# A gated recurrence and a long convolution on one core: row-tiled transposes and single-bank PSUM outputs

## The chip, the cores and the metric

The kernel runs on one core of one Trainium2 chip. The metric is device time in microseconds (us) for one launch. The core has five engines that run their own instruction streams: TensorE (PE, matrix multiply, with its weight loads shown apart as PEld), VectorE (DVE), ScalarE (ACT), GpSimd (POOL) and SyncE (SP, which here issues all DMAs). Matmul results land in PSUM, 8 banks of 512 fp32 values in each of 128 partitions; PE alone writes matmul outputs there, and in this kernel ACT and DVE read ("evict") them. A weight load puts the stationary operand into PE's array. An operand of 64 rows takes one half of the array's rows, a "row tile"; two row tiles can work side by side.

## The reference

Four batches of 6272 steps and 256 channels; all inputs and the output are fp32.

```python
sig = 1 / (1 + exp(-f_logit))
f = lower_bound + (1 - lower_bound) * sig
i = 1 - f
for t in range(S):                       # per batch and channel
    h = f[:, t] * h + i[:, t] * x[:, t]
    y[:, t] = h
proj = y @ w_proj                        # 256 -> 768
x1, x2, x3 = proj[..., :D], proj[..., D:2*D], proj[..., 2*D:]
X2 = rfft(x2, axis=1)
H = rfft(filter_fft, axis=0)
x2_conv = irfft(X2 * H, axis=1)
out = (x1 * x2_conv * x3) @ w_out
```

## The kernel before

The sequence of 6272 is split as 128 x 49, and the Fourier transforms are done as matmuls with small tables: a transform over 128, then one over 49, with the twiddles folded into a shifted table. The work of one batch has these steps, each with the name that the code gives its operations:

- `hgrn(b)`: 13 chunks of 512 steps (the last 128). A chunk's `x` and `f_logit` are loaded with time on the partitions, four blocks of 128 steps. ACT makes the sigmoid in place (`sig`, line 392), POOL multiplies `u = x * sig` in place (`u`, line 394), PE transposes both to channels on the partitions (`sT` of the gate, `uT` of u, line 401), for each half `kh` of the channels apart. ACT turns the transposed gate into f (`f`, line 415), and DVE runs the recurrence with a scan instruction that reads f from SBUF and u from PSUM (`scan`, line 423). A copy of the first 3072 steps is put behind the end (`wrap`).
- `phase_p`: x2, projected straight into the order that the transform needs (`P`, line 730; evicted by `x2`, line 733).
- `phase_f1`: the transform over 128, units of 8 channel pairs, 16 units a batch (`F1`, line 743; evicted by `A`, line 746). `mini` does the same few rows of all units at once.
- `unit`: the transform over 49 in two row tiles of 64 (`F2`, line 788), the product with the filter's spectrum on DVE (`prod`, line 801, two an unit, one for each of the two banks o = 0, 1), a small POOL add (`slot`), and the inverse over 49 (`I2`, line 811; evicted by `Th`, line 816).
- `gate`: x1 and x3 in 13 chunks and two halves of the channels (`x13`, line 450), copied to SBUF by ACT (`xs`, line 462) and multiplied on POOL into `zt` (`z`, line 466).
- `phase_o`: 13 groups of four of the 49 residues (the last group one): the inverse over 128 in two row tiles (`I1`, line 844), the product with `zt` on DVE (`y`, line 850), the output projection (`proj`, line 862), its eviction (`o`, line 868) and the store.

A preparation ahead of the first batch makes the tables and the filter's spectrum with the same two transforms (`rot`, `FF1` at line 672 with its eviction `afs`, `FF2`), and runs `hgrn(0)` beside them. `hgrn(b+1)` is put in after `phase_o(b)` in the program, and its operations mix with those of batch b.

The order of all instructions is not the program's order. Each step calls `op(...)`, which records an operation with its inputs and outputs, the engines that may do it with a cost in us for each, and, for a matmul group, the number of neighbouring PSUM banks that it takes (`take`). `Plan.schedule` then lists the operations by simulated time: it takes the operation that could start earliest, with ties by `levels` (the longest way to the end) plus two hand-set tables, `LEAD` and `TILT`; `SHY` adds a delay to an engine's offer for a kind of operation. `ROWS` names the kinds that run in row tiles, and `STICK` makes PE prefer to stay on one side. A bank is free again when all readers of the operation that took it are done, or, where the readers name a `part`, bank by bank. `either(n)` offers ACT and DVE for an eviction of n elements a partition. At run time every engine runs its list in order, and waits on semaphores for data and banks.

Of the kernel before, what the change touches and what calls it, by code (L numbers as in the profile page):

```python
# [10 lines left out]
F32R = mybir.dt.float32r  # L11
F16 = mybir.dt.float16
I32 = mybir.dt.int32
AOP = mybir.AluOpType
# [43 lines left out]
class Plan:  # L58
# [14 lines left out]
    SHY = {("A", "ACT"): 27, ("A", "DVE"): 27, ("Th", "ACT"): -10, ("Th", "DVE"): 779,  # L73
            ("afs", "ACT"): 51, ("afs", "DVE"): -12, ("f", "ACT"): -4, ("f", "DVE"): 452,
            ("f2", "ACT"): 100, ("f2", "DVE"): 126, ("fr", "ACT"): 290, ("fr", "DVE"): 2705,
            ("fr", "POOL"): -84, ("hw", "ACT"): -32, ("hw", "DVE"): 364, ("o", "ACT"): 13,
            ("o", "DVE"): 1968, ("wrap", "ACT"): 1376, ("wrap", "POOL"): 115, ("x2", "ACT"): 90,
            ("x2", "DVE"): 63}

    STICK = 4.0  # L80
    ROWS = ("F2", "mini", "I1", "FF2", "last")
# [3 lines left out]
        "A": (10, -421, 208, -185), "F1": (-87, -1, 1, -163), "F2": (297, -97, -22, -362),  # L85
        "FF1": (-72, 0, 0, 0), "FF2": (-79, 0, 0, 0), "H": (-184, 334, 22, 133),
        "I1": (-280, -65, -92, 13), "I2": (-282, -43, -206, 0), "P": (-10, -2, 64, -49),
        "Th": (-3, -372, 21, -100), "afs": (-31, 0, 0, 0), "f": (-348, -382, -7, -601),
        "f2": (206, 0, 0, 0), "ff": (-455, 0, 0, 0), "fr": (-21, 0, 0, 0), "hst": (-91, 0, 0, 0),
        "hw": (11, 0, 0, 0), "load": (-7, -238, -192, 0), "mX": (18, 0, 0, 0),  # L90
        "mini": (-412, 357, -19, 94), "o": (0, -19, 214, 0), "pad": (14, 0, 0, 0),
        "prod": (0, -199, -22, 1135), "proj": (387, -1338, -11, 254), "rot": (-287, 0, 0, 0),
        "sT": (-25, 1516, -37, 149), "scan": (-40, -6, -71, -138), "sig": (-116, 262, -46, -451),
        "slot": (-6, -10, -78, 18), "store": (-23, -498, 174, 242), "tabs": (335, 0, 0, 0),
        "u": (-6, 0, -48, 383), "uT": (-1369, -27, 23, 104), "warm": (-427, 0, 0, 0),
        "wrap": (0, 312, 253, 2), "x13": (-140, -373, -471, -159), "x2": (35, -288, 339, 160),
        "xs": (2160, 1264, 0, 301), "y": (-27, 470, 49, -42), "z": (0, 0, 532, 756),
        "zm": (1130, 0, -12, 65),
# [3 lines left out]
        "A": (35, -373, 1648, 137), "F1": (462, -629, 1502, 4000), "F2": (5639, 140, 319, 1412),  # L102
        "FF2": (-1269, 0, 0, 0), "H": (0, -477, -796, -1751), "I1": (-67, 978, 15, 184),
        "I2": (-35, -8, 4207, 55), "P": (-34, -342, 3292, -57), "Th": (164, 540, 125, 0),
        "args": (598, 0, 0, 0), "f": (294, -69, -69, -264), "f2": (-491, 0, 0, 0),
        "ff": (5684, 0, 0, 0), "fr": (505, 0, 0, 0), "hst": (566, 0, 0, 0), "hw": (-475, 0, 0, 0),
        "iden": (346, 0, 0, 0), "iota": (33, 0, 0, 0), "last": (43, 0, 0, 0),
        "load": (1910, -587, 70, -424), "mX": (103, 0, 0, 0), "mini": (162, -443, 3560, 2034),
        "o": (182, 252, -11, 418), "pad": (-134, 0, 0, 0), "pre": (-656, 0, 0, 0),
        "prod": (53, -700, 0, 7), "proj": (-7749, -9436, -6234, 114), "rest": (109, 0, 0, 0),  # L110
        "sT": (0, -96, -2, -1), "scan": (-892, 17, -1191, -2973), "sig": (0, 79, 43, 146),
        "slot": (126, 219, 502, 1379), "store": (-387, -299, -79, -369), "tabs": (5294, 0, 0, 0),
        "turns": (-46, 0, 0, 0), "u": (801, 3, 107, 648), "uT": (10, -692, -6798, -121),
        "warm": (-40, 0, 0, 0), "wcol": (443, 0, 0, 0), "wl": (-474, 0, 0, 0),
        "wrap": (-936, -549, -39, 333), "x13": (-350, -2412, -46, -1943), "x2": (0, 0, 1048, 2601),
        "xs": (5528, -104, 106, -88), "y": (-100, -570, -30, -285), "z": (-742, -2, 69, 0),
        "zm": (236, 148, 847, -6),
# [41 lines left out]
    def schedule(self, level):  # L159
# [14 lines left out]
        base = {}  # L174
# [13 lines left out]
        while base:  # L188
            rooms = {n: self.room(bank, n) for n in (1, 2)}
            best = None  # L190
            for i, b in base.items():
# [8 lines left out]
                for e, a in b.items():  # L200
                    a = max(a, floor, free[e])
                    c = a + (o["cost"][e] * 0.01 if len(b) > 1 else 0.0)
                    c += self.SHY.get((o["kind"], e), 0) / 100
                    stick = self.STICK if e == "PE" and (o["kind"] in self.ROWS) == rows else 0.0
                    key = (c, -level[i] - stick, i, e, a)
                    if best is None or key < best:
                        best = key
# [32 lines left out]
            for j in inform.get(i, ()):  # L240
                wait[j] -= 1
            for j in o["succ"]:
# [35 lines left out]
def kernel(  # L278
# [65 lines left out]
    def At(u):  # L344

        return [("At", u % NA)]
# [33 lines left out]
    def hgrn(b):  # L380
        for c in range(NCHK):
# [6 lines left out]
            for dst, src, t in ((ft, f_logit, ("ft", k)), (xt, x, ("xt", k))):  # L388
# [5 lines left out]
            op("u", {"POOL": 0.1 + 0.553 * nb}, lambda e, xt=xt, ft=ft: nc.gpsimd.tensor_tensor(  # L394
                xt, xt, ft, op=AOP.mult), r=[("ft", k)], w=[("xt", k)])
            for kh in range(2):
# [537 lines left out]
```

## Time and profile before

| | |
|---|---|
| five runs | 503.39 to 510.31 us, median 506.26 |
| profiled execution | 507.04 us, of which the span from the first to the last instruction is 505.2 |
| mean granted PE clock | 0.991 of full speed |
| DMA | 116.39 MB, 230 GB/s on average over the span |

| group, by line | count | mean ns | busy us |
|---|---|---|---|
| L466 POOL z (128x490) | 96 | 1983 | 189.0 |
| L801 DVE prod | 128 | 1198 | 146.7 |
| L394 POOL u (128x1024) | 48 | 2384 | 114.3 |
| L423 DVE scan (128x512) | 96 | 1270 and 1218 | 120.2 |
| L401 PE transposes, 128x128 f32 | 784 | 283 and 276 | 124.7 |
| L401 PE weight loads for them | 784 | 142 | 90.9 |
| L862 PE projection, 128x256 | 392 | 292 | 59.2 |
| L862 PE weight loads for it | 392 | 188 | 49.6 |
| L850 DVE y (128x1024) | 48 | 1216 | 58.0 |
| L415 ACT f (128x512) | 96 | 694 | 66.6 |
| L462 ACT x1s and x3s (128x490) | 192 | 591 | 113.3 |
| L462 ACT x1s and x3s (128x392) | 16 | 508 and 506 | 8.1 |
| L361 ACT Th (128x784) | 64 | 824 | 52.7 |
| L363 ACT o (128x1024) | 48 | 1024 | 49.0 |
| L361 ACT A (128x1024), L366 DVE A | 46, 18 | 1024, 1216 | 46.9, 21.6 |
| L361 ACT f2, L366 DVE f2 (128x512, strided read of PSUM) | 13, 11 | 688, 697 | 7.8, 7.1 |
| L366 DVE afs (128x512) | 32 | 677 | 20.8 |
| L707 PE weight loads (64x98 fp32r) | 8 | 162 | 0.5 |

How to read it: a row's mean is the time from an instruction's start to its modelled end, while the next one on the engine may already have started, above all on PE, where a row of 283 ns does not mean that PE is taken for 283 ns. In the chain of waits an instruction counts only until the next in the chain starts. "L450 <- L811" style releasers are inferred from semaphore events. PEclk is the granted clock; it stood at full speed from 90 us on.

### The profile page before, as it was taken

What the parts mean: (1) busy time and instruction counts of PE and PEld (TensorE: products, weight loads), DVE (VectorE), ACT (ScalarE), POOL (GpSimd) and SP (SyncE); (2) the same over time, 40 slices, a digit from 0 to 9 for tenths busy, and PEclk for the clock granted to TensorE, in tenths of its full rate; (3) what the DMA queues carried; (4) which work ended last, traced back from release to release, by engine and by line L of the source; (5) the groups of instructions that cost most, each with busy time, mean ns of one, the idle gap of its engine ahead of it and who ended that gap; (6) DMA issues with size and microseconds to landing.
All of it is one profiled execution on the core that took longest, in us unless ns stands there. A gap on an engine that the chain in (4) does not pass through costs nothing. (4 is left out here: it accounts for less than half of the span.)

```text
span 505.2 us, 13245 instructions
## 1 busy us (share of the span) xinstructions
PE 479.7 (95%) x5257; PEld 374.5 (74%) x5257; DVE 444.0 (88%) x451; ACT 411.5 (81%) x587; POOL 386.1 (76%) x328
## 2 busy tenths in 40 slices
PE   7979998999999999999998999999999999999795
PEld 6768785866777899867766889767778888666484
DVE  8789997789899999899996989989999978989773
ACT  3657867889999877899898787899989777999654
POOL 8886766789999864499999867789998732997900
PEclk9998999999999999999999999999999999999999
DMA  8969999616668999247678899056788970344166
GB/s 331 407 216 287 322 309 302 208 39 217 219 204 272 280 321 393 96 134 215 194 212 273 290 328 361 9 172 205 242 284 300 334 281 28 97 128 133 62 240 272
DMA packets 41725, 116.39 MB, mean 230 GB/s; under 512 B 4384, under 2 KB 6304, under 8 KB 41664
## 3 DMA queue, kind: packets, MB, share of 16 engines
q1 hardware_dynamic: 41664, 115.56, 67.6%
q8 instruction: 41, 0.67, 0.6%
q14 instruction: 20, 0.16, 0.1%
HBM read 84.54 MB, written 31.00 MB: 229 GB/s over the span
## 5 line engine op out<-in xcount | busy, mean ns | idle before, releaser
L466 POOL TENSOR_TENSOR zt<-x1s,x3s 128x490 f16<-128x490 f32 (+1 forms) x104 | 201.8, 1954 | 42.6 <-ACT x3s L462 26.1
L801 DVE TENSOR_TENSOR PP<-PS,Hu 98x1008 f16<-98x1008 f32 x128 | 146.7, 1198 | 10.1 <-ACT x3s L462 3.3
L394 POOL TENSOR_TENSOR XT<-XT,FL 128x1024 f32<-128x1024 f32 (+1 forms) x52 | 117.2, 2257 | 34.5 <-DMA XT<-in_x_dram 13.5
L423 DVE TENSOR_TENSOR_SCAN HA<-fTs,HA,PS 128x512 f16<-128x512 f32 (+1 forms) x96 | 114.0, 1203 | 12.3 <-PE PS L401 8.2
L450 PE MATMUL PS<-HA,W 128*128 128x490 f16 (+1 forms) x416 | 107.8, 372 | 1.8 <-DVE PP L801 1.0
L415 ACT ACTIVATE fTs<-PS,nomc 128x512 f32<-128x512 f32 (+1 forms) x104 | 69.5, 669 | 19.9 <-PE PS L401 12.9
L850 DVE TENSOR_TENSOR ys<-PS,zt 128x1024 fp32r<-128x1024 f32 (+1 forms) x52 | 59.9, 1158 | 12.9 <-PE PS L844 8.0
L363 ACT ACTIVATE osb<-PS 128x1024 f32<-128x1024 f32 (+1 forms) x52 | 50.6, 977 | 20.3 <-PE PS L862 17.5
L401 PE MATMUL PS<-iden,XT 128*128 128x128 f32 x392 | 63.5, 283 | 3.2 <-ACT fTs L415 1.5
L462 ACT ACTIVATE x1s<-PS 128x490 f32<-128x490 f32 (+1 forms) x104 | 60.8, 585 | 5.8 <-PE PS L450 2.9
L462 ACT ACTIVATE x3s<-PS 128x490 f32<-128x490 f32 (+1 forms) x104 | 60.6, 584 | 3.9 <-POOL zt L466 2.1
L862 PE MATMUL PS<-Wo,ys 128*128 128x256 f32 x392 | 59.2, 292 | 2.9 <-DVE ys L850 1.7
L401 PE MATMUL PS<-iden,FL 128*128 128x128 f32 x392 | 61.2, 276 | 0.3 <-ACT FL L392 0.3
L811 PEld LDWEIGHTS <-PP 98*128 98x128 f16 x1024 | 50.1, 98 | 10.8 <-issue 2.4
L392 ACT ACTIVATE FL<-FL 128x1024 f32<-128x1024 f32 (+1 forms) x52 | 52.6, 1013 | 6.1 <-DMA FL<-in_f_logit_dram 6.0
L401 PEld LDWEIGHTS PS<-iden,XT 128*128 128x128 f32 x392 | 45.1, 142 | 15.7 <-POOL XT L394 2.6
L361 ACT CAST Th<-PS 128x784 f16<-128x784 f32 x64 | 52.7, 824 | 4.6 <-PE PS L811 4.2
L450 PEld LDWEIGHTS <-W 128*128 128x128 f16 x416 | 35.2, 99 | 28.1 <-issue 10.3
L862 PEld LDWEIGHTS PS<-Wo,ys 128*128 128x128 f32 x392 | 49.6, 188 | 7.1 <-DVE ys L850 2.2
L811 PE MATMUL PS<-VA,PP 98*128 98x98 f16 x512 | 52.4, 207 | 1.5 <-DVE PP L801 0.7
L811 PE MATMUL PS<-VB,PP 98*128 98x98 f16 x512 | 52.1, 207 | 0.0
L366 DVE CAST X<-PS 128x1024 f16<-128x1024 f32 (+1 forms) x34 | 46.9, 1476 | 5.2 <-PE PS L730 3.9
(98 smaller groups left out, 699.9 us busy)
## 6 DMA issues: line engine op xcount, KB each, us to landing
Hu<-H SPq DMA_DIRECT2D x64, 392.0 KB
FL<-in_f_logit_dram SPq DMA_DIRECT2D x48, 512.0 KB
XT<-in_x_dram SPq DMA_DIRECT2D x48, 512.0 KB
out_dram<-osb SPq DMA_DIRECT2D x48, 512.0 KB
X<-in_moe_filter_fft_dram SPq DMA_DIRECT2D x9, 512.0 KB
H<-Hu SPq DMA_DIRECT2D x16, 196.0 KB
H<-Hu SPq DMA_DIRECT2D x16, 128.0 KB
Hu<-in_moe_filter_fft_dram SPq DMA_DIRECT2D x2, 512.0 KB
```

Of the source, the lines that this page charges most:

```text
L361: nc.scalar.copy(dst, src)
L394: op("u", {"POOL": 0.1 + 0.553 * nb}, lambda e, xt=xt, ft=ft: nc.gpsimd.tensor_tensor(xt, xt, ft, op=AOP.mult), r=[("ft", k)], w=[("xt", k)])
L401: nc.tensor.transpose(PS[:, p, j:128 * nb:nb], src[:, j, cols], iden[:])
L415: nc.scalar.activation(fT, PS[:, p, 0:n], AF.Identity, scale=by, bias=1.0)
L423: nc.vector.tensor_tensor_scan(h, fT, PS[:, p, 0:n], init, op0=AOP.mult, op1=AOP.add),
L450: nc.tensor.matmul(PS[:, p, 0:n], W13[:, kh, js], HA[:, HB[kh] + t0:HB[kh] + t0 + n], start=(kh == 0), stop=(kh == 1))
L462: nc.scalar.activation(xs(i), PS[:, p, 0:n], AF.Copy, scale=1.0 if i else ZS),
L466: nc.gpsimd.tensor_tensor(late["zt"][:, jb, :, m0:m0 + nm], xs(0).rearrange("p (m r) -> p r m", r=Q), xs(1).rearrange("p (m r) -> p r m", ...
L801: nc.vector.tensor_tensor(PP[:TB, k, o, :, :, 1:64], px.unsqueeze(1).broadcast_to([TB, 2, UE, 63]), hh[:, :, :, 1:64], op=AOP.mult)
L811: nc.tensor.matmul(PS[:, ib + o, pr * TB:(pr + 1) * TB], PP[:TB, k, o, n, 2 * pr:2 * pr + 2, :], v[:TB], start=(n == 0), stop=(n == 1))
L850: nc.vector.tensor_tensor(late["ys"][:, yk, :, 0:rn * 128], PS[:, cb:cb + 2, 0:rn * 128], late["zt"][:].rearrange("p k r m -> p k (r m)") ...
L862: nc.tensor.matmul(po[:, i, :], late["ys"][:, yk, kh, i * 128:(i + 1) * 128], Wo[:, kh, :], start=(kh == 0), stop=(kh == 1))
```

## The change

It does the following.

- A 128x128 transpose is done as two of 64 rows (`turn`), one in each row tile, each with a 64x64 identity. One operation `sT` (and one `uT`) now serves both halves of the channels: it takes two neighbouring banks, the first row tile writes the last n columns of the first bank and the second row tile the first n of the second, and the halves of the channels interleave. `f` and `scan` read every second column of that run. `sT` and `uT` are added to `ROWS`.
- `F1`, `I2` and `proj` are split in halves of one bank each, with an eviction for each half. `A`, `Th` and `osb` get a token for each half, so a half of I2 needs only its own prod.
- `FF1`'s table `D1r` is no longer doubled; the matmuls stream 128 columns in place of 256, and a group takes one bank.
- `u` and `z` may be done by DVE as well as POOL, `xs` by DVE as well as ACT.
- The planner remembers for an operation that takes banks when its readers' other inputs are ready (`need`), and delays the operation's offer until its result is due then.
- The tables `SHY`, `TILT` and `LEAD` have new values, and so the order of the instructions is another one everywhere.

```diff
-    SHY = {("A", "ACT"): 27, ("A", "DVE"): 27, ("Th", "ACT"): -10, ("Th", "DVE"): 779,
...
+    JIT = 0.0
-    ROWS = ("F2", "mini", "I1", "FF2", "last")
+    ROWS = ("F2", "mini", "I1", "sT", "uT", "FF2", "last")
...
+                    if o["take"]:
+                        c = max(c, need[i] - o["cost"][e] - self.JIT)
...
             for j in inform.get(i, ()):
                 wait[j] -= 1
+                need[j] = max(need[j], end[i] + self.LAT[e])
...
-        return [("At", u % NA)]
+        return [("At", u % NA, h) for h in range(2)]
...
-            op("u", {"POOL": 0.1 + 0.553 * nb}, lambda e, xt=xt, ft=ft: nc.gpsimd.tensor_tensor(
+            op("u", {"POOL": 0.1 + 0.553 * nb, "DVE": 0.07 + 0.268 * nb}, lambda e, xt=xt, ft=ft: (nc.gpsimd if e == "POOL" else nc.vector).tensor_tensor(
                 xt, xt, ft, op=AOP.mult), r=[("ft", k)], w=[("xt", k)])
+            def run(p, at, m, step):
+
+                return PS[:, p:p + 2].rearrange("m a n -> m (a n)")[:, at:at + (m - 1) * step + 1:step]
+
+            def turn(e, p, src, nb=nb, n=n, run=run):
+                for j in range(nb):
+                    for kh in range(2):
+                        for a in range(2):
+                            rows = slice(64 * a, 64 * a + 64)
+                            nc.tensor.matmul(run(p, 512 - n + a * n + kh + 2 * j, 64, 2 * nb),
+                                             src[rows, j, kh * 128:kh * 128 + 128], iden[rows, rows],
+                                             is_transpose=True, start=True, stop=True)
+            sT = op("sT", {"PE": 0.125 * nb}, lambda e, p, f=turn, s=ft: f(e, p, s),
+                    r=[("ft", k), "iden"], w=["qT"], take=2)
+            uT = op("uT", {"PE": 0.125 * nb}, lambda e, p, f=turn, s=xt: f(e, p, s),
+                    r=[("xt", k), "iden"], w=["qT"], take=2)
             for kh in range(2):
-                def turn(e, p, src, cols=cols, nb=nb):
-                    for j in range(nb):
-                        nc.tensor.transpose(PS[:, p, j:128 * nb:nb], src[:, j, cols], iden[:])
-                sT = op("sT", {"PE": 0.109 * nb}, lambda e, p, f=turn, s=ft: f(e, p, s),
-                        r=[("ft", k), "iden"], w=["qT"], take=1)
-                uT = op("uT", {"PE": 0.109 * nb}, lambda e, p, f=turn, s=xt: f(e, p, s),
-                        r=[("xt", k), "iden"], w=["qT"], take=1)
...
-                        nc.scalar.activation(fT, PS[:, p, 0:n], AF.Identity, scale=by, bias=1.0)
+                        nc.scalar.activation(fT, run(p, at, n, 2), AF.Identity, scale=by, bias=1.0)
...
-                   nc.vector.tensor_tensor_scan(h, fT, PS[:, p, 0:n], init, op0=AOP.mult,
+                   nc.vector.tensor_tensor_scan(h, fT, run(p, at, n, 2), init, op0=AOP.mult,
...
-                    op("xs", {"ACT": 0.05 + n / 1200.0}, lambda e, p, xs=xs, n=n, i=i:
+                    op("xs", {"ACT": 0.05 + n / 1200.0, "DVE": 0.07 + n / 960.0}, lambda e, p, xs=xs, n=n, i=i:
...
-                op("z", {"POOL": 0.1 + 3.68 * n / 1000}, lambda e, xs=xs, jb=jb, m0=m0, nm=nm:
-                   nc.gpsimd.tensor_tensor(
+                op("z", {"POOL": 0.1 + 3.68 * n / 1000, "DVE": 0.08 + 1.7 * n / 1000},
+                   lambda e, xs=xs, jb=jb, m0=m0, nm=nm:
+                   (nc.gpsimd if e == "POOL" else nc.vector).tensor_tensor(
...
-        D1r = tmp.tile([128, 2, 128], F32R, name="D1r")
+        D1r = tmp.tile([128, 128], F32R, name="D1r")
...
-                        w=[("FF1", u, h)], take=2)
+                        w=[("FF1", u, h)], take=1)
...
-        f1 = op("F1", {"PE": 0.056 * UE}, mm, r=[("x2", g) for g in range(NX2)] + ["D1"], take=2)
-        k = u % NA * UE
-        op("A", either(1024), lambda e, pb: copy(
-            e, A[:, k:k + UE],
-            PS[:, pb:pb + 2].rearrange("p a (i r k) -> p (a i) r k", r=2, k=64)),
-           w=At(u), src=f1)
+        for h in range(2):
+            k = u % NA * UE + 4 * h
+
+            def mm(e, pb, j=u * UE + 4 * h):
+                for i in range(4):
+                    nc.tensor.matmul(PS[:, pb, i * 128:(i + 1) * 128], X2[:, (j + i) * PW:(j + i) * PW + 128],
+                                     D1[:], start=True, stop=True)
+            f1 = op("F1", {"PE": 0.224}, mm, r=[("x2", g) for g in range(NX2)] + ["D1"], take=1)
+            op("A", either(512), lambda e, pb, k=k: copy(
+                e, A[:, k:k + 4], PS[:, pb].rearrange("p (i r k) -> p i r k", r=2, k=64)),
+               w=[("At", u % NA, h)], src=f1)
...
-        i2 = op("I2", {"PE": 0.695}, inv,
-                r=[("P", k, 0), ("P", k, 1), ("Pz", k, 0), ("Pz", k, 1), "V"], take=2)
-        op("Th", either(784), lambda e, ib: copy(
+            i2 = op("I2", {"PE": 0.347}, inv, r=[("P", k, o), ("Pz", k, o), "V"], take=1)
+            op("Th", either(392), lambda e, ib, o=o: copy(
...
-            po = op("proj", {"PE": 0.259 * rn}, proj, r=[("y", yk)], take=2)
+            for i0 in range(0, rn, 2):
+                n = min(2, rn - i0)
...
+                po = op("proj", {"PE": 0.259 * n}, proj, r=[("y", yk)], take=1)
+                op("o", either(256 * n), lambda e, ob, k=k, i0=i0, n=n: copy(
```

## The prediction

> **What bounds the kernel now.** I read the page's first part, then the busy time by stage, then the chain of waits inside one stage, then the groups by shape. The columns of the stage table are us from the start, length, and busy us (x instructions) of PE, PEld, DVE, ACT and POOL, then clock, DMA share and GB/s. Its cuts are the first matmuls of each batch's P (line 730): preparation with the first recurrence, three middle stages (one batch's spectrum, gate and output, beside the next batch's recurrence), and a last stage with no recurrence beside it.
>
> ```profile
> PE 479.7 (95%) x5257; PEld 374.5 (74%) x5257; DVE 444.0 (88%) x451; ACT 411.5 (81%) x587; POOL 386.1 (76%) x328
> ```
>
> ```profile
> 0.00:90.20 90.20, 80.67 (x580) 63.58 (x581) 74.98 (x108) 61.58 (x84) 66.11 (x85) 0.96 0.90 312
> 90.20:200.40 110.20, 108.39 (x1245) 85.68 (x1244) 102.59 (x95) 96.93 (x141) 93.48 (x69) 1.00 0.71 235
> 200.40:307.50 107.10, 102.99 (x1195) 80.53 (x1194) 97.52 (x92) 90.75 (x132) 86.31 (x66) 1.00 0.70 228
> 307.50:414.10 106.60, 105.59 (x1227) 83.83 (x1226) 99.06 (x93) 93.64 (x137) 87.62 (x67) 1.00 0.68 234
> 414.10:505.20 91.10, 82.02 (x1018) 60.91 (x1016) 69.80 (x65) 68.62 (x96) 52.60 (x42) 0.99 0.41 142
> ```
>
> A busy PE is a modelled thing, so its prices come from the chain of waits in a stretch where PE alone is the chain (start, us, what):
>
> ```profile
> 379.68 0.87 PE PS L401 x8
> ...
> 382.61 1.01 PE PS L844 x32
> ...
> 386.49 0.56 PE PS L844 x16
> 387.04 1.02 PE PS L401 x8
> 388.07 0.95 PE PS L862 x8
> 389.01 0.56 PE PS L844 x16
> ```
>
> Eight transposes (L401) take 0.87, or 0.109 each. Sixteen more I1 matmuls (L844, two row tiles of 64) cost 1.01 - 0.56 = 0.45, or 0.028 each; what is left of 0.56 is 0.11, the price of leaving row tiles for the full array. Coming back costs 1.02 - 0.87 = 0.15 at most. A projection matmul is 0.95 / 8 = 0.118. The same chain gives P 0.109 (x98 in 10.74), x13 0.206 (x8 in 1.65), F1 0.056 (x24 in 1.34), F2 0.54 for eight with a switch in it, I2 0.044 (x16 in 0.70).
>
> PE's load in a middle stage, summed: P 98 x 0.109 = 10.7; x13 104 x 0.206 = 21.4; F1 128 x 0.056 = 7.2; F2 16 x 0.54 = 8.6; I2 256 x 0.044 = 11.3; I1 196 x 0.028 = 5.5; projection 98 x 0.118 = 11.6; transposes 196 x 0.109 = 21.4; together 97.7. The order of PE's records shows about 62 switches a stage, of which F2's 16 are already counted; 46 x 0.1 = 4.6. Sum 102 of 106.6 us: PE is 96% taken, so PE sets the middle stages. DVE and ACT stand close behind (99.1 and 93.6 us busy of 106.6).
>
> **The change part by part.** The sum is made against the profiled execution, 507.04 us (span 505.2 and 1.8 around it); the median of the five runs, 506.26, is 0.8 less.
>
> *Transposes.* A 128x128 transpose becomes two of 64 rows, in two row tiles and two banks. Per 128 rows of one tensor, two instructions of 0.109 become two pairs. What is a pair worth? The rows that bear on it:
>
> ```profile
> 82.48 0.71 PE L690 MATMUL PS<-afs,FTr 64*98 64x512 f32 x4
> 83.02 0.48 PE L707 MATMUL PS<-mX,FTr 64*98 64x128 f32 x8
> 83.44 0.66 PE L401 MATMUL PS<-iden,XT 128*128 128x128 f32 x4
> ```
>
> L707 is the nearest: fp32r in two row tiles, eight matmuls between 83.02 and 83.44. Less the switch of 0.1 that is four pairs in 0.32, so 0.08 a pair, though each loads its own weights of 98 columns and streams 128. Low bound: half as many streamed columns, 0.055 a pair. High bound: the load alone sets the 0.109 and doesn't shrink with half the rows, 0.109 a pair, gain nothing. Between them: the load row of L707 lasts 160 ns and its pair 83, of the projection 188 ns and its step 118, so a load row is 70 to 77 ns longer than what it costs; the transposes' load row is 142 ns, which leaves 65 to 72. I take 0.07 a pair: it comes from three rows of fp32 loads. A middle stage has 196 transposes, so 196 x (0.109 - 0.07) = 7.6 us of PE; by the bounds 0 to 10.6.
> The Trainium skill (TensorE: Matmul & The Clock Gate, "LDWEIGHTS") says the opposite of my choice: a load takes columns / 1.2 GHz whatever its rows, 107 ns for 128 columns, so the pair would stay at 0.107 and the gain at zero; L707's pair at 0.08 for 98 columns agrees with that rule as well as with mine.
>
> *Switches.* The transposes now stand on the row-tiled side. Counted in the same order of PE's records, a middle stage would have 78 to 88 switches in place of 62 to 64, +20 x 0.1 = 2 us; an order that groups them can avoid some. I take 1.6. Net of PE: 6 us a stage, to 96; at the same 96% share the stage would last 100.6.
>
> *F1, I2, projection in halves.* The same matmuls on PE, but 44 more evictions a batch (16 A, 16 Th, 12 o). ACT rows at two sizes give the fixed part: 490 elements 591 ns, 392 elements 506 ns (L462), so 0.87 ns an element and 165 ns fixed. The chain shows neighbours on ACT 0.47 apart where the row says 0.59, so only some 45 ns of that is lost between neighbours. 44 x 0.045 to 44 x 0.165 is 2 to 7 us, shared by ACT and DVE; I take 3. They stand idle for 13.0 and 7.5 us of the stage at 106.6, and what a shorter stage takes from that is the limit I give below. In return each half's reader starts a matmul group earlier, and the second half of I2 needn't wait for the first's eviction; that fills gaps, and I count it at nothing (0 to 1 us a stage).
>
> *Strided reads.* f and scan now read every second element of two banks. The nearest rows are the f2 copies, which read PSUM 256 elements apart: ACT 688 ns for 512 against 694 for the contiguous f, DVE 697 against 677 for afs. At most 20 ns x 26 on either engine, 0.5 us a batch; taken as zero. The strided write goes from every fourth to every eighth element; no row prices it, and it is inside the pair's bounds.
>
> *FF1.* 128 columns in place of 256. Its step is the load's, 0.118 as in L862, and L707's pairs show that 128 fp32r columns need no more than 0.08. Taken as zero, bounds -3 to +3 us in the preparation, where DMA (0.90 busy) and DVE hide it.
>
> *z, u and xs also on DVE.* POOL's z is 1983 ns and u 2384. On DVE, z is bounded by half a prod (1198 / 2 = 0.6) and by POOL's own 1.98; u is nearest to y (1216). In the middle stages DVE has no room to take many. The last stage is different:
>
> ```profile
> 473.84 3.33 POOL zt L466 x2
> 477.17 1.54 POOLq L929
> 478.73 1.24 DVE ys L850
> 480.00 1.21 PE PS L862 x8
> ```
>
> From 467.1 to 477.2 the chain is POOL's z, while PE is busy 11.0 of the 14 us from 466 to 480. DVE has 3.3 us free there. Taking a few z off POOL can bring the output forward by no more than PE's idle 3.0; I take 3 (0 to 4). The twelve output groups after it are PE's, I1 0.56 and projection 1.14, and stay.
> The skill (Advanced Engine Details and Errata, "GPSIMD Details") says that POOL shares a port with DVE and conflicts with DVE instructions of two SBUF inputs, which z and u on DVE would be; no DVE row here has two large SBUF inputs. By it, this part would be worth nothing.
>
> *Preparation.* The first recurrence saves the same 7.6 us of PE less switches, but DMA is 0.90 busy and DVE 75.0 of 90.2; I take 2 (0 to 5).
>
> *Sum.* 3 x 6 + 3 + 2 = 23: 507.0 - 23 = 484, on the median 483; I write 483.5.
>
> What is late next: DVE and ACT. Per stage they are busy 192.7 of 213.2 us; with 3 more and a stage of 100.6, 195.7 of 201.2. It just fits, because a busy row contains up to 0.12 us in which the next instruction already runs, and only if A, x2 and xs are spread evenly. If it doesn't fit, a stage saves 2 to 3 us, not 6.
>
> **The rivals.**
> *DVE and ACT take over.* For it: scans and y's alternate on DVE in the output stretch, 1270 + 1216 ns, against PE's group of 0.56 + 0.95 + 1.02 = 2.53, so there DVE is already level with PE and the transposes' gain is worth nothing in it. Against: recurrence and evictions can move between stretches. 3 x 2.5 + 2 = 9.5: 497.
>
> *The pair costs what the whole did.* A load of 128 columns sets the pace, PE saves nothing, switches cost 3 x 2 and the tail gives 3 back: 507 + 6 - 3 = 510. For it: the high bound above. Against: load rows of 142 for a step of 109.
>
> *Banks held longer: slower.* One chunk's sT and uT now hold two banks each until both of their readers are done; before, a bank was free after one reader. With I1's two and the projection's two, the eight are full: the next chunk's transposes can start only after the second scan, and DVE then waits for them: 8 pairs x 0.07 + 0.15 + about 0.1 of hand-over = 0.8 us a chunk (scans already wait on L401 0.63 on average, 8.8 us in 14 waits). It decides from 23 / 0.8 = 29 of the 52 chunks on, for then it has eaten the gain. With 45 chunks uncovered, +36 - 23: 520. Against: y (1.22) can stand between two chunks' scans, and sT's banks are free after two f of 0.69.
>
> **How the numbers follow.** Forecast 484: 0.66. Engines take over, 497: 0.12. Pair at full price, 510: 0.12. Banks, 520: 0.10. The forecast's own range: pairs at 0.055, no extra switches and 5 and 4 at the two ends make 3 x 9 + 9 = 36, so 471; 3 x 2.5 + 1 makes 498. The range that leaves out two in ten reaches over the second case and into the third: 470 to 507. A change of 1% is about what the runs can tell from none: faster 0.77, same 0.12, slower 0.11.
>
> **What would show it.** In the profile after: sixteen half transposes in about 0.56 us in the chain (0.44 or 0.87 would be the bounds); PE's share falling while DVE and ACT reach 95% of a middle stage; stages near 101 us; POOL's z gone from the chain before the last output. Wrong would be: scans waiting on L401 at most chunks; stages still at 106 with PE's row tiles at 0.109 a pair; or ACT's idle time before its evictions gone while PE waits for free banks.

## The result, and the profile after

| | before | after |
|---|---|---|
| median of the runs (lowest to highest, number) | 506.61 (503.39 to 510.31, 43) | 515.89 (506.35 to 523.13, 24) |
| ratio to before, 95% interval | | 1.0078 [1.0049, 1.0108] |
| profiled execution, and its span | 507.04, 505.2 | 514.09, 512.0 |
| mean granted PE clock of the profiled execution | 0.991 | 0.972 |

The change made the kernel slower, by 0.8% in the ratio and by 9 us in the medians; forecast were 483.5, and 470 to 507 as the range. The ratio leaves out the longest runs of after, in which the granted clock was lowest, so it is smaller than that of the medians, 1.018; the low clock turns out to be part of the change's effect. The page's busy row, the slices of PE and of its clock, after:

```profile
PE 466.2 (91%) x6041; PEld 352.4 (69%) x6041; DVE 453.0 (88%) x470; ACT 425.1 (83%) x758; POOL 363.4 (71%) x314
...
PE   8888987899799898999999979999999999999996
...
PEclk9996598999899999999999999999999999999999
```

PE is no longer at 95%, so something was taken off it; and the fourth and fifth slices, near 38 to 64 us, show a clock near half, which before did not have. The chain of waits after (start, us, what) shows what the transposes cost now:

```profile
47.62 1.90 PE PS L410 x32
...
306.87 1.01 PE PS L410 x32
...
336.52 0.98 PE PS L800 x16
337.50 0.49 PE PS L410 x16
338.00 1.35 PE PS L463 x6
```

Sixteen half transposes, eight pairs, take 0.49, or 0.061 a pair against 0.109 for the whole one before. At 47.62, in the slow stretch, 32 take 1.90, nearly twice the 1.01 of 306.87. The windows by stage, cut at the first matmul of each batch's P (start:end, length, busy us of PE, PEld, DVE, ACT, POOL, then clock, DMA share, GB/s):

```profile
0.00:94.30 94.30, 80.18 (x806) 62.12 (x806) 72.95 (x111) 66.78 (x93) 68.97 (x86) 0.87 0.87 304
94.30:206.80 112.50, 102.86 (x1400) 77.16 (x1400) 103.13 (x96) 96.94 (x178) 81.89 (x64) 0.98 0.69 227
206.80:318.00 111.20, 101.76 (x1431) 76.81 (x1430) 103.81 (x99) 96.48 (x179) 86.09 (x66) 1.00 0.70 231
318.00:421.10 103.10, 97.35 (x1370) 72.42 (x1369) 99.24 (x93) 92.31 (x171) 77.50 (x62) 1.00 0.70 222
421.10:512.00 90.90, 84.03 (x1042) 63.92 (x1038) 73.84 (x75) 72.62 (x140) 49.00 (x39) 0.99 0.43 151
```

Cut at the same places, before has 90.3, 105.6, 111.5, 106.5 and 91.2 us (the second cut of the prediction's table, 200.40, belongs at 195.9; the sum of the first two middle stages is hardly touched). So preparation lost 4.0, the first middle stage lost 6.9, the third gained 3.4, and the others stayed. PE is idle for some 9.5 us in each of the first two middle stages (before 1.8 and 4.1): the time that was taken off it became gaps.

Two things stand out. One is the clock: in the rows of 3.4 us from 45.4 to 62.4 it is at exactly half. The windows of one such row, before and after:

```profile
48.80:52.20 3.40, 3.35 (x26) 2.75 (x27) 3.05 (x5) 2.02 (x3) 2.25 (x3) 1.00 0.90 259
```

```profile
48.80:52.20 3.40, 3.40 (x26) 2.65 (x23) 2.63 (x3) 3.02 (x4) 1.82 (x4) 0.50 0.75 204
```

PE is just as "busy" in both; the busy row says nothing of the clock. In the whole profiled execution the half-speed stretches of after are 20.5 us from 42.7 and 3.4 each at 83.6 and 131.4; before has 3.4 each at 38.8 and 86.6 (both have one more at the end). The other thing is VectorE. Its timeline and that of POOL after, and a piece of the chain of waits farther on (start, us, engine, line, operation):

```profile
121.75 2.30 DVE L813 TENSOR_TENSOR PP<-PS,Hu 98x1008 f16<-98x1008 f32 x2
123.96 4.33 DVE L399 TENSOR_TENSOR XT<-XT,FL 128x1024 f32<-128x1024 f32 x1
128.21 1.27 DVE L436 TENSOR_TENSOR_SCAN HA<-fTs,HA,PS 128x512 f16<-128x512 f32 x1
```

```profile
122.70 0.65 POOL L376 COPY HA<-HA 128x512 f16<-128x512 f16 x1
123.27 3.93 POOL L479 TENSOR_TENSOR zt<-x1s,x3s 128x490 f16<-128x490 f32 x2
129.54 1.16 POOL L376 COPY HA<-HA 128x512 f16<-128x512 f16 x2 [2.34 <-DVE HA L436]
```

```profile
314.98 0.63 DVE XT L399
315.61 1.46 issue
317.07 0.84 DVE HA L436 x2
317.92 2.02 DVE zt L479
```

A `u` on VectorE takes 4.33 us, and ends 1.09 after POOL's two z's end at 127.20: it stood on the engine until POOL was done with both. The shortest u of this size takes 1.23 (at 30.02, beside a memset of POOL); the four others stand beside z's of POOL, take 1.56 to 4.33, and each ends 1.08 or 1.09 after the end of a z. The 14 rows of u and z on DVE sum to 23.5 us, where the planner's costs make 13.0. Behind the long u waits the scan, behind the scan POOL's own next copy (2.34 idle); PE stands idle for 2.59 from 128.04, and at 131.4 the clock dips. In the chain's piece from 314.98 a u and a z of DVE stand in the chain itself.

### The profile page after: what moved, and what is told of

It reads as the page before. It is cut to its first block, busy times and chain, and to the rows that moved or that the text cites. A ratio compares the mean times of both kernels' runs of the same rounds, so it can differ in the third digit from the quotient of the medians.

```text
span 512.0 us, 15070 instructions
## 1 busy us (share of the span) xinstructions
PE 466.2 (91%) x6041; PEld 352.4 (69%) x6041; DVE 453.0 (88%) x470; ACT 425.1 (83%) x758; POOL 363.4 (71%) x314
## 4 chain that ended last, share of the span: by engine, by line
PE 46%; ACT 16%; DVE 12%; POOL 10%; issue 8%; DMA 6%; ACTq 0%; SPq 0%; DVEq 0%; POOLq 0%
PE PS L463 8%; PE PS L877 7%; PE PS L742 6%; PE PS L410 5%; POOL zt L479 5%; PE PS L823 4%; PE PS L800 4%; PE PS L756 4%; PE PS L855 4%; POOL XT L399 3%; DVE HA L436 3%; ACT fTs L428 3%; DVE X L371 2%; PE PS L683 2%; DVE PP L813 2%
## 5 line engine op out<-in xcount | busy, mean ns | idle before, releaser
L479 POOL TENSOR_TENSOR zt<-x1s,x3s 128x490 f16<-128x490 f32 (+1 forms) x96 | 189.6, 1991 | 57.2 <-DVE ys L861 34.0
L399 POOL TENSOR_TENSOR XT<-XT,FL 128x1024 f32<-128x1024 f32 (+1 forms) x46 | 104.8, 2278 | 41.2 <-ACT FL L397 24.0
L463 PE MATMUL PS<-HA,W 128*128 128x490 f16 (+1 forms) x416 | 105.6, 371 | 0.8
L368 ACT ACTIVATE osb<-PS 128x512 f32<-128x512 f32 (+1 forms) x100 | 54.1, 592 | 22.7 <-PE PS L877 14.4
L428 ACT ACTIVATE fTs<-PS,nomc 128x512 f32<-128x512 f32 (+1 forms) x104 | 64.4, 667 | 8.1 <-PE PS L410 4.0
L366 ACT CAST Th<-PS 128x392 f16<-128x392 f32 x128 | 61.3, 529 | 4.4 <-PE PS L823 4.3
L366 ACT CAST HA<-PS 128x512 f16<-128x512 f32 x101 | 56.7, 618 | 5.3 <-PE PS L756 4.5
L823 PE MATMUL PS<-VA,PP 98*128 98x98 f16 x512 | 56.3, 208 | 1.5 <-POOL PP L805 0.9
L823 PE MATMUL PS<-VB,PP 98*128 98x98 f16 x512 | 55.8, 207 | 0.0
L742 PE MATMUL PS<-W,HA 128*128 128x256 f16 x392 | 45.9, 273 | 2.7 <-DVE X L371 1.9
L410 PE MATMUL PS<-iden,XT 64*128 64x64 f32 x784 | 38.1, 236 | 11.2 <-POOL XT L399 3.3
## 6 DMA issues: line engine op xcount, KB each, us to landing
FL<-in_f_logit_dram SPq DMA_DIRECT2D x48, 512.0 KB
XT<-in_x_dram SPq DMA_DIRECT2D x48, 512.0 KB
out_dram<-osb SPq DMA_DIRECT2D x48, 512.0 KB
X<-in_moe_filter_fft_dram SPq DMA_DIRECT2D x9, 512.0 KB
Hu<-in_moe_filter_fft_dram SPq DMA_DIRECT2D x2, 512.0 KB
```

What stands on the lines that cost most here:

```text
L366: nc.scalar.copy(dst, src)
L368: nc.scalar.activation(dst, src, AF.Copy, scale=scale)
L399: op("u", {"POOL": 0.1 + 0.553 * nb, "DVE": 0.07 + 0.268 * nb}, lambda e, xt=xt, ft=ft: (nc.gpsimd if e == "POOL" else nc.vector).tensor_t ...
L410: nc.tensor.matmul(run(p, 512 - n + a * n + kh + 2 * j, 64, 2 * nb), src[rows, j, kh * 128:kh * 128 + 128], iden[rows, rows], is_transpose ...
L428: nc.scalar.activation(fT, run(p, at, n, 2), AF.Identity, scale=by, bias=1.0)
L463: nc.tensor.matmul(PS[:, p, 0:n], W13[:, kh, js], HA[:, HB[kh] + t0:HB[kh] + t0 + n], start=(kh == 0), stop=(kh == 1))
```

## The experiments

All times are medians, ratios are to runs of before on the same chip (their medians were 506.8 to 507.7). "Own order" means that every engine's list is the one of the kernel named, only the instructions' content differs. The theories: the clock falls because PE streams too little; PE's time is not what sets the end, since the other engines are as tight; u and z on VectorE hurt, or are needed to relieve POOL; the loads hide the gain; and last, the order itself. The statements on record number them as they came up.

**The parts of the change, in after's own order.** Three kernels:

```diff
# a1_wide: FF1 streams 256 columns again in three of four matmuls
-                    for i in range(4):
-                        nc.tensor.matmul(PS[:, pb, i * 128:(i + 1) * 128],
-                                         f2[:, (j + i) * PW:(j + i) * PW + 128], D1r[:],
+                    for i, w in enumerate((2, 2, 2, 1)):
+                        nc.tensor.matmul(PS[:, pb, i * 128:(i + w) * 128], f2[:, (j + i) * PW:(j + i) * PW + 128],
+                                         D1r[:, 0:w].rearrange("m x k -> m (x k)"),
...
# a2_pool: every u and z on POOL, at its place in the order
-        for i, e, b in self.schedule(level)[1]:
+        for i, e, b in [(i, "POOL" if self.ops[i]["kind"] in ("u", "z") else e, b) for i, e, b in self.schedule(level)[1]]:
# a3_full: whole transposes, one bank for each half of the channels, contiguous reads; FF1 stays at 128 columns
+                        nc.tensor.transpose(PS[:, p + kh, j:128 * nb:nb], src[:, j, kh * 128:kh * 128 + 128], iden[:])
...
```

> The changed kernel in its own order, but FF1 streams 256 columns in three of each four matmuls (the surplus 128 are written over by the next one), as the kernel before did. Theory 1, the clock: the changed PE streams too little in the preparation, FF1's halved width being the largest part of that, so the half-speed stretch of about 20 us at 38 to 58 us shrinks to one of 3.4 us; mean clock back to 0.985 or more, and 4 to 8 us less than the changed kernel. Theory 2, the evictors: PE's clock is beside the point because DVE and ACT set the pace; within 2 us of the changed kernel, whatever the clock does.

> The changed kernel in its own order, with all u and z done by POOL (the planner's places for them kept; 6 u and 8 z leave DVE). Theory 2: u on DVE took up to 4.3 us in the changed profile where y's row suggested 1.2, and POOL's z beside it up to 3.0 where it takes 2.0; taking them off DVE gives back part of 13 us of DVE and is 2 to 8 us faster. Theory 3, POOL needs the relief: the recurrence's u come later on POOL, and it is 2 to 8 us slower. Theory 1: within 2 us.

> The changed kernel in its own order, with the transposes done as before: one 128x128 transpose for each block and half of the channels, in a bank for each half; f and scan read a whole bank without a step. PE has some 36 us more to do. If PE still sets the pace, as my prediction held, it is 20 to 36 us slower than the changed kernel. Theory 2: PE has about 10% to spare, so less than 12 us slower. Theory 1: it streams more, so the clock stays up in the preparation (0.99) and that gives 4 us back there.

| kernel | us | ratio | clock in its profile |
|---|---|---|---|
| a1_wide | 510.80 (506.00 to 516.15) | 1.0061 [1.0027, 1.0095] | 0.988 |
| a2_pool | 522.62 (517.61 to 527.84) | 1.0269 [1.0220, 1.0318] | 0.953 |
| a3_full | 515.62 (512.09 to 518.89) | 1.0162 [1.0115, 1.0208] | 0.991 |

Streaming 256 columns, more work of no use, takes 5 us off the median (515.9 to 510.8), and the half-speed stretch of 20.5 us is gone (three of 3.4 are left): the clock is a cause. It shows in the medians and in the clock over all runs (median 0.974 and 0.990), hardly in the two ratios, 1.0078 and 1.0061. In this order POOL can't take all u and z back; it becomes later and the clock falls further. With whole transposes PE has 36 us more to do by the planner's costs (784 transposes at 0.109 against 392 groups of two pairs at 0.125). a3_full stands 4.8 us above a1_wide, though the two differ in FF1's width as well; a12_ld_full below repeats the comparison with FF1 wide in both. The stage windows of a1_wide and a3_full, first two middle stages each, show where the 36 us go.

```profile
91.20:200.30 109.10, 101.89 (x1400) 76.55 (x1400) 101.05 (x96) 96.74 (x178) 82.71 (x64) 1.00 0.70 234
200.30:311.10 110.80, 101.56 (x1430) 76.75 (x1429) 104.03 (x99) 96.27 (x179) 85.94 (x66) 1.00 0.71 233
```

```profile
91.70:202.40 110.70, 106.36 (x1215) 82.86 (x1213) 101.10 (x96) 96.68 (x178) 82.61 (x64) 1.00 0.69 228
202.40:314.80 112.40, 107.65 (x1226) 84.15 (x1225) 103.51 (x98) 96.92 (x178) 85.77 (x66) 1.00 0.69 231
```

The stages differ by 1.6 us each. With whole transposes PE fills its gaps (106 to 108 busy), with pairs it has them (102); DVE and ACT do the same work in the same time in both (101 to 104 and 96 to 97 us busy).

**The narrow FF1 alone, in the order of before.** b1_narrow streams 128 columns in FF1 and keeps the rest.

> The kernel before in its own order, with FF1 streaming 128 columns, nothing else changed. Theory 1: the clock falls to half speed for longer than 3.4 us in the preparation, and the time rises by 3 to 8 us. Theory 2: within 1 us of the kernel before, as FF1's step is its weight load's.

506.58, ratio 0.9993 [0.9964, 1.0021], profile's clock 0.991. By itself it does nothing. In the order of after the long half-speed stretch needed both narrowings: with FF1 wide it is gone (a1_wide), and a3_full, whose transposes are whole while FF1 is narrow, also entered half speed at 42.8 but was back after 3.4 us; after stayed for six such lengths. The median clocks over all runs go the same way: 0.974 for after, 0.990 for a1_wide, 0.993 for a3_full. What the clock answers to isn't shown. a1_wide kept full speed in the same stretch, with PE busy for less of it:

```profile
48.80:52.20 3.40, 2.47 (x21) 1.85 (x20) 3.17 (x4) 2.23 (x4) 0.87 (x3) 1.00 0.89 274
```

So rows that were busy throughout did not bring the clock back in after, and a row with 0.93 of idle time did not lower it in a1_wide. Nor does the streamed share tell the two kernels apart, by an estimate from F1's 128 columns in 0.056 at full speed (24 in 1.34) and each matmul's share of the 128 rows: the half-speed rows of after stream 0.26 to 0.31 of what PE could at full speed, and the half-speed row of before, from 38.8, some 0.28, yet before was back at full speed after it. At half the clock no row can exceed 0.5, so these figures can't say which came first.

**Taking work off one engine.** In the order of before: x13 with one of its two matmuls (b6_x13: x1 and x3 lack half of their sum; 208 matmuls of 0.206, so PE -43 us), z on half its elements for one half of the channels from the second batch on (b7_z, POOL -38), xs on half its columns (b8_xs, ACT -31), y on half its elements (b9_y, DVE -21), all four (b10_all). And with a1_wide, y on half its elements (a8_yhalf, DVE -27).

```diff
# b6_x13
-                        for kh in range(2):
+                        for kh in range(1):
...
# b9_y, a8_yhalf (with w = 64)
-                   late["ys"][:, yk, :, 0:rn * 128], PS[:, cb:cb + 2, 0:rn * 128],
+                   late["ys"][:, yk, :, 0:rn * w], PS[:, cb:cb + 2, 0:rn * w],
...
```

> The kernel before in its own order, with x13 summed over one half of the channels only (the second matmul of each pair is left out, so x1 and x3 are half sums). It takes 104 x 0.206 / 2 = 10.7 us of PE off each batch, 43 us in all, about what the transposes' change takes off, and nothing off DVE, ACT or POOL. Theory 0, my prediction's: PE sets the middle stages, so it is 15 to 35 us faster than the kernel before. Theory 2, DVE and ACT stand level with PE: 2 to 12 us faster.

> The changed kernel in its own order, with FF1 wide as in a1_wide, and y made for half of its elements only (the other half of ys stays at a zero that is written once); PE does the same work. It takes 13 x 0.53 = 6.9 us of DVE off each batch, 27 us in all. Theory 2: DVE sets the pace of the changed kernel, so it is 10 to 25 us faster than a1_wide's 511. Theory 0: PE sets it, 0 to 6 us faster.

> The kernel before in its own order; from the second batch on z multiplies half of its elements for the first half of the channels (the rest of zt keeps the first batch's values). It takes 39 x 1.0 = 38 us off POOL and nothing off the others. Theory 4: POOL sets the spectrum stretches, where it is busy ten tenths in many 10-us windows, and the kernel is 12 to 30 us faster. Theory 2 as it stands after the last runs, four engines level and each alone worth little: 0 to 8 us faster.

> The kernel before in its own order; from the second batch on x1 and x3 are copied by ACT for half of their columns only (the buffers keep older values). It takes 156 x 0.2 = 31 us off ACT alone. Theory 2: 0 to 8 us faster. Theory 5, ACT sets the pace: 10 to 25 us faster.

> The kernel before in its own order; from the second batch on y is made for half of its elements (ys keeps older values). It takes 39 x 0.53 = 21 us off DVE alone. Theory 2: 0 to 6 us faster. DVE as the sole bound: 12 to 21 us faster.

> The kernel before in its own order with all four relieved at once: x13 over half of the channels, z, xs and y as in the runs b7_z, b8_xs and b9_y (43 us off PE, 38 off POOL, 31 off ACT, 21 off DVE). Theory 2: what one engine gives up shows only when the others give it up too; 18 to 30 us faster, clearly more than the sum of the four single runs. If the pace is set by something that none of these touch (DMA, or waits from one engine to the next), 12 us or less, no more than the single runs' sum.

| kernel | relieved | us | ratio |
|---|---|---|---|
| b6_x13 | PE 43 | 501.87 (498.89 to 505.14) | 0.9906 [0.9873, 0.9940] |
| b7_z | POOL 38 | 505.94 (504.98 to 510.42) | 0.9967 [0.9925, 1.0008] |
| b8_xs | ACT 31 | 506.44 (503.24 to 508.19) | 0.9972 [0.9950, 0.9995] |
| b9_y | DVE 21 | 505.33 (501.99 to 507.51) | 0.9950 [0.9920, 0.9980] |
| b10_all | all | 494.49 (491.01 to 495.90) | 0.9725 [0.9680, 0.9770] |
| a8_yhalf | DVE 27 | 509.84 (503.41 to 511.10) | 1.0029 [0.9992, 1.0066] |

b6_x13 is the prediction's premise by itself: 43 us off an engine that is 95% busy are worth 5. None of the other three engines is the bound in its place; each gives 1 to 2 us (of b7_z and b8_xs the intervals reach 1.0008 and 0.9995, so hardly more than nothing). All four give 13, little more than the sum of the singles, 5.3 + 1.6 + 1.1 + 2.2 = 10, and less than was expected. The busy row of b10_all:

```profile
PE 451.1 (91%) x5049; PEld 358.6 (73%) x5049; DVE 424.2 (86%) x451; ACT 382.5 (77%) x587; POOL 352.9 (71%) x328
```

With 133 us of steps taken out of four engines none is above 91%, and DVE, ACT and POOL have fallen to 86% and less. No engine's share is the bound here either. By elimination, what is left is the time of chains that run through all of them, in an order that was made for other durations, and the loads, which b10_all doesn't relieve (b11_ld below).

**Split evictions.** b5_split does each A, Th and o of before as two instructions, 176 more.

> The kernel before in its own order, with each eviction of A, Th and o done as two instructions, one for each bank; the matmuls, banks and waits stay. It adds 44 evictions a batch, 176 in all. My prediction priced them at 2 to 7 us a batch on ACT and DVE together, of which the end would show little: 1 to 5 us slower. Theory 2, the evictors are as full as PE: 5 to 12 us slower. Theory 1, the clock: no change of it, so nothing from that.

504.89, ratio 0.9974 [0.9942, 1.0006]: the cost that was put at 3 us a batch isn't there.

**The loads.** b11_ld (before) and a11_ld (a1_wide) load half of the partitions of x and f_logit from the second batch on; a12_ld_full is a11_ld with whole transposes. The other half of those values is not refreshed.

> The kernel before in its own order; from the second batch on, each load of x and f_logit fetches 64 of the 128 partitions (the other rows keep older values). 12.8 MB of a batch's 25.6 MB of loads and stores become 6.4 less. Theory 6: DMA, busy 0.9 to 1.0 of the output stretches, sets their pace: 6 to 20 us faster. Theory 2, all engines level and DMA not among them: 0 to 4 us faster.

> The changed kernel in its own order with FF1 wide, and loads halved as in b11_ld. Theory 6: DMA hides what the transposes gave, so this is 10 to 25 us faster than a1_wide's 511. Theory 2: 0 to 5 us faster.

> As a11_ld, with the transposes as whole 128x128 ones. Theory 6: with DMA out of the way the 36 us of PE show, and this is 12 to 30 us slower than a11_ld. Theory 2: it stays within 8 us of a11_ld, as a3_full did of a1_wide (5).

b11_ld 502.08, ratio 0.9900 [0.9861, 0.9939]; a11_ld 510.74, 1.0053 [1.0019, 1.0086]; a12_ld_full 515.56, 1.0166 [1.0129, 1.0203]. In the order of before, halving the loads is worth 5.7 us, as much as 43 us of PE; the prediction counted DMA in the preparation only. In the order of after it is worth nothing in the median, with a lower clock (median 0.983, a1_wide 0.990), some 3 us with the clock set aside as below; the 10 to 25 that one theory expected are excluded, so the loads aren't where the gain went. Whole transposes cost 4.8 us here, with FF1 wide in both.

**VectorE's u and z without POOL.** a13_onein is a1_wide with those 6 u and 8 z as instructions of one SBUF input.

```diff
-                       xs(0).rearrange("p (m r) -> p r m", r=Q),
-                       xs(1).rearrange("p (m r) -> p r m", r=Q), op=AOP.mult),
+                       ... if e == "POOL" else nc.vector.tensor_scalar(late["zt"][:, jb, :, m0:m0 + nm], in0=xs(0).rearrange("p (m r) -> p r m", r=Q), scalar1=1.0, scalar2=None, op0=AOP.mult),
```

> The kernel after in its own order, with FF1 streaming 256 columns as in a1_wide, and with the 6 u and 8 z that VectorE does replaced there by one-input instructions of the same output size (u: a scaled copy through a strided view; z: a strided copy of x1s). It leaves out these 14 multiplications, and nothing else. Theory 7 (POOL and DVE shut each other out while either does a two-input instruction from SBUF, and the 14 rows on DVE cost the chain about 9 us beyond their planned time): no such DVE row above about 2.4 us, POOL's rows beside them back at 1.98 and 2.38, and a time of 502 to 507, against 510.8 for a1_wide. Rival (the long rows are hidden like everything else in this kernel): 509 to 512.

507.77 (502.91 to 510.82), ratio 1.0009 [0.9969, 1.0049]: 3 us below a1_wide, above the first range and below the rival's. The groups by shape on DVE (busy, mean ns), after and a13_onein, and a line of a13_onein's DVE timeline:

```profile
L399 DVE TENSOR_TENSOR XT<-XT,FL 128x1024 f32<-128x1024 f32 x5 | 11.9, 2386 | 0.4 <-ACT FL L397 0.4
...
L479 DVE TENSOR_TENSOR zt<-x1s,x3s 128x490 f16<-128x490 f32 x6 | 9.0, 1493 | 0.4 <-ACT x3s L368 0.2
```

```profile
L399 DVE TENSOR_SCALAR XT<-XT 128x1024 f32<-128x1024 f32 x5 | 9.2, 1837 | 0.0
...
L481 DVE TENSOR_SCALAR zt<-x1s 128x490 f16<-128x490 f32 x6 | 6.6, 1099 | 0.1
```

```profile
118.68 2.48 DVE L399 TENSOR_SCALAR XT<-XT 128x1024 f32<-128x1024 f32 x1
120.89 1.34 DVE L436 TENSOR_TENSOR_SCAN HA<-fTs,HA,PS 128x512 f16<-128x512 f32 x1
```

The experiment did less than it was meant to: a one-input instruction from SBUF to SBUF waits for POOL as well. The u at 118.68 began 0.69 after a z of POOL and takes 2.48; the shortest of this size takes 1.32, and a one-input z takes 0.60 alone (at 82.35), but 1.68 and 1.79 beside a z and a u of POOL (at 307.38 and 316.12). The waits became shorter, they did not go: the 14 rows sum to 18.0 us, against 21.6 in a1_wide. The time fell by about as much as they did (3.0 us in the medians). So these rows seem to stand on the path nearly in full, which y's don't (a8_yhalf); the intervals of a1_wide and a13_onein overlap, and a kernel without any of these waits in this order wasn't tried.

**An order of its own.** In the kernel's planner before ends at 485 and after at 480; the measured medians stand 22 and 36 us above. Two kernels put this to use: a4_tuned has the change with wide FF1 and with u and z on POOL only, and new `SHY`, `TILT` and `LEAD`, found by random search on the planner's own end (481.3); b3_tuned is before with single banks alone, searched in the same way (481.9). a14_tuned2 is a4_tuned searched further (479.4).

> The changed kernel with FF1 wide, u and z on POOL alone, and SHY, TILT and LEAD set anew for that by a random search on the planner's own end time, so another order (the planner's end: 481 us; 480 for the changed kernel and 485 for the one before). Theory 7: u and z on DVE wait for POOL and cost the changed order some 8 us that the planner doesn't see, and the clock the rest; then this one is 2 to 10 us faster than the kernel before. If the relief of POOL was worth it after all, or the planner's end says nothing at this scale, it is no faster than a1_wide's 511.

> The kernel before with one part of the change only, single banks for F1, I2 and the projection with an eviction for each; transposes stay 128x128, u, z and xs stay where they were; a new order from tables searched on the planner's own end, 481.9. With a4_tuned (the same, with row-tiled transposes and the planner's wait added, planned 481.3) it shows what the transposes are worth once each version has an order of its own. Theory 8 (PE's share is no bound, so transposes that are half as long bring little; single banks and the order bring what there is): 501 to 506, within 2 of a4_tuned. Rival (the shorter transposes are worth their 36 us of PE in part, and a4_tuned's gain is theirs): 507 to 514.

> a4_tuned again with tables searched further, the planner's end at 479.4 in place of 481.3; nothing else differs. If the time follows the plan (measured less planned was 22.3 for a4_tuned and 22.5 for before): 500.5 to 503.5. Rival (below about 2 us the plan says nothing, and orders of equal plans differ by several us on the chip): anything from 500 to 510.

| kernel | us | ratio |
|---|---|---|
| a4_tuned | 503.55 (501.63 to 508.51) | 0.9934 [0.9907, 0.9961] |
| a14_tuned2 | 504.72 (499.73 to 506.67) | 0.9937 [0.9899, 0.9975] |
| b3_tuned | 506.94 (504.02 to 510.07) | 1.0013 [0.9973, 1.0052] |

a4_tuned is faster than before by 0.7%, and than after by 1.4%. Between it and b3_tuned, of nearly equal plans, stand the half transposes (and the planner's new wait): 0.8%, some 4 us, so "within 2 us" was missed. That the transposes are the reason isn't shown by this pair alone, as the two orders differ too. a14_tuned2, two us shorter by the plan, gained nothing, so a difference of this size in the plan doesn't tell orders apart.

## Why the prediction was wrong

The step that failed is "PE is 96% taken, so PE sets the middle stages", with "at the same 96% share the stage would last 100.6" after it. The share was right and no bound followed from it. PE's 102 us of work stood among DVE's 99 and ACT's 94 in an order in which each engine waits for the others; the relieved PE waits for the others instead, 19.1 us in the first two middle stages against 5.9 before. Shown: b6_x13 (43 us off PE for 5), and whole against half transposes in one order (a12_ld_full to a11_ld, 4.8). Two less clean pairs agree: a3_full to a1_wide, 4.8, with another FF1, and b3_tuned to a4_tuned, about 4, in another order. So some 36 us of PE are worth about 5 in the medians, an eighth; with the clock set aside as below the first two pairs give 9 and 7, good to some 3, so a fifth to a quarter. The prediction had 18 us in the middle stages come through whole. Of its signs of being wrong, the waits of scans at most chunks and pairs at 0.109 didn't come: it had no sign for a share that is no bound. (At the same share, 96 us of PE would make a stage of 100.3; 100.6 is 106.6 less 6. And its best case has 9 a stage where its own bound of 0.055 gives 10.6. Neither decides anything.)

What turned this gain of 5 into a loss of 9 in the medians is seen best with the clock set aside. A straight line through each kernel's run times against their mean clocks gives, at a clock of 0.990: before 508.0 (121 runs), after 510.1, a1_wide 510.5, a13_onein 506.5, a4_tuned 502.3, a14_tuned2 502.2; the slopes are 3 to 5 us for 0.01 of clock, and the fits are good to some 2 us for after and 1 for the others.

- The clock: 515.9 - 510.1 = 6. After's median clock over its runs is 0.974, that of before 0.992. Shown by a1_wide, with the stretch in the profile; why the clock fell is open. The prediction had FF1 at nothing, -3 to +3, by its steps on PE, and had no term for the clock; the preparation, which should have saved 2, lost 4.0, and 0.9 with a1_wide.
- u and z on VectorE: 510.5 - 506.5 = 4 for rows that became 3.6 us shorter in a13_onein; about 6 us of waits are still in them (18.0 less 14 such rows at their shortest, 11.6). The prediction took 3 for this part as a gain in the tail. The tail's own step was half right: POOL's z is gone from the chain before the last output, but a z on DVE (1.27 from 484.86) and xs stand there instead, and the last stage went from 91.2 to 90.9. The Trainium skill (Advanced Engine Details and Errata, "GPSIMD Details"), which the prediction quoted against itself, names this conflict over a shared port; the rows of u agree, 4.33 us the longest, and show it as a wait for the end of POOL's z.
- The rest: from a13_onein's 506.5 to a4_tuned's 502.3 are 4 more, with the same transposes and banks. In them are the waits that were left and the order of after, which isn't as good on the chip as its plan of 480 says. The two weren't separated.

The other terms:

- The pair was put at 0.07, bounds 0.055 to 0.109; it is 0.061. The Trainium skill (TensorE: Matmul & The Clock Gate, "LDWEIGHTS (loading the stationary operand)") lets a load take columns / 1.2 GHz whatever its rows, an estimate of 107 ns for 128 columns. A single load's row does not get shorter with half the rows (median 138 ns against 140), as it says; but a pair of them follows the next in 61, so what the prediction drew from the rule, a pair at 0.107, is not what a pair costs here.
- Switches: 20 more a stage were forecast; PE's records show 280 before and 344 after, 16 more for each of the four recurrences.
- Split evictions: 3 us a batch forecast, none measured (b5_split). Strided reads: scans are at 1267 against 1270; nothing, as forecast.
- The first rival, DVE and ACT take over, named the right kind of thing at the wrong price: relief of DVE alone by 27 us, in a8_yhalf, gave 1 to 2 us (3 with the clock set aside). The second, the pair at full price, is excluded. The third, banks held longer, ended near the measured time by chance: scans wait for transposes 9.6 us in 11 waits, before 8.8 in 14.

## What to carry to other kernels

Before an engine's share of busy time is taken for the bound, take some of its work out in the same order and see what the end does: with three engines between 81% and 95% in an interleaved, fixed order, an eighth of the relief was all that arrived. An operation between SBUF operands wasn't free to move from POOL to VectorE while POOL did others of that kind: each waited for the other's whole instruction, and so did all that was queued behind. And look at the granted clock, not only at the busy row, when columns are saved where PE isn't the bound: here saved columns cost the clock.

## What the hardware showed unexpectedly

The granted clock fell to half and stayed there for 20.5 us though PE was busy in 3.40 of 3.40 us of each row from 45.4 to 62.4. In the row ahead of it, 39.3 to 42.7, PE was busy for 1.91 of 3.40, with 1.49 as its longest idle time. 256 columns in place of 128 at one line, or whole transposes, took the long stretch away. The Trainium skill (TensorE: Matmul & The Clock Gate, "HAM oscillation — how this bites in real kernels") puts its rule as no idle gaps of PE above about 3.4 us; here no gap of that length was there, so the rule is not enough for this case. The runs don't show what is.

An instruction of VectorE between two SBUF operands waits for all of POOL's running z, and once waited for the next one too (4.33 us for a u that otherwise takes 1.23); POOL's next z then waits for it (3.0 us in place of 1.98, at 316.00 for one). One-input instructions with strided views waited as well (2.48). And 64x128 fp32 weight loads into two row tiles come 0.061 us a pair, less than one row of them lasts (138 ns).
